# First block of one token tile, late first global queries, held weight joins, and stacked value parts in an attention and MLP kernel

## The chip, the cores and the metric

The kernel runs on one core of a Trainium2 chip. The metric is the device time of one execution in microseconds, as the median over runs. The core has TensorE (PE; its weight loads are listed apart as PEld), VectorE (DVE), ScalarE (ACT), GpSimd (POOL) and SyncE (SP), which here issues every data transfer.

## The reference

Sparse attention is followed by a two-layer MLP, both in float32 (the MLP weights arrive as 64-bit floats).

```
# 8 sequences b, 8 heads, 512 local tokens (l), 32 global tokens (g), head size 64
k_all = concat([k_g, k_l]); v_all = concat([v_g, v_l])
out_g = softmax(q_g @ k_all.T / 8) @ v_all          # a global query sees all 544 keys
s_ll  = where(|i - j| <= 32, q_l @ k_l.T / 8, -1e9)  # a local query sees a band
out_l = softmax(concat([q_l @ k_g.T / 8, s_ll])) @ concat([v_g, v_l])
x = heads of concat([out_g, out_l]) side by side     # 8 * 544 = 4352 tokens x 512
h = x @ w_in                                         # 512 -> 2048
return (h * sigmoid(h)) @ w_out                      # 2048 -> 512
```

## The kernel before

The 4352 tokens are 34 tiles of 128: for each half of the sequences, four sequences of four local tiles (chunk `c` of 0 to 3 in sequence `b`), and one tile with the global tokens of these four sequences. `SIZES` groups the tiles into blocks for the MLP: 2, ten times 3, and 2.

**MLP.** `first_layer(n, f)` makes 128 of the 2048 hidden columns for all tiles of block n, in PSUM tile `h`; ACT (tanh) and DVE make the activation; `second_layer(n, f)` adds its product with `w_out` to one PSUM bank `out` per tile. f runs over 16, and the second layer of a pass comes after the first layer of the next. Block 0 multiplies whole float32 values (`w_32`, `xh`). From block 1 on, each operand is split in a high part (rounded to fp32r, a faster form of TensorE) and a low part (the rest), and three products are made for one: high·high, high·low, low·high (L563, L588 to L590).

**Weights.** `load_weights` (L164) takes half of one f's weights: SP fetches 512 KB of 64-bit words into `raw_w` (a ring of eight), ACT makes the float from the upper word (L179), DVE shifts the lower word (L181) and joins both (L182). `split_weights` (L185) makes `w_hi` on ACT (L192) and `w_lo` on POOL (L193). It is called in block 0's `second_layer`, after the last use of the whole weights of that f. `LOOK` and `FIRSTW` set how many passes ahead the loading runs.

**Attention** comes in 128 steps, k = 16 b + 4 c + pr, each of two heads (u) and one local tile:

- `st_load`, `st_vload` fetch queries, keys and values; `st_split`, `st_vsplit` split them;
- `st_scores` makes the scores `s` on PE and the softmax on DVE and ACT into `probs`; split steps send these through a DMA into `rr`, which gives them the fp32r type;
- `st_turn` transposes them on PE into `t`, from where ACT and DVE write `pt` (or `pt_hi`, `pt_lo`). Beside the 128 columns of local queries stand 32 columns of global queries, which POOL copies from `pgt` (L398 to L402);
- `st_out` multiplies values and `pt` into PSUM tile `o`: 160 columns are 128 local and 32 global queries (L423). A split step makes, for each head and each half `a` of the keys, three products on 64 stationary columns: `vhi`·`pt_hi`, `vlo`·`pt_hi` and `vhi`·`pt_lo`. ACT copies the high part to `xh` (L434), DVE the rest to `xl` (L435) and the sum over chunks of the global part to `acc` (L440, L442).

Steps below `KF` = 24 work on whole float32 values in transposes and outputs, and below 24 also in the scores; steps 24 to 27 (`ND` = 28) split a compact layout in which the two heads are stacked on the 128 rows.

**Global queries.** For sequence b, `g_load`, `g_split`, `g_scores` (tile `gs`, four pairs of heads), `g_soft` (softmax in `pgs`) and `g_turn` (transposes into `pgt`, parts `gt` and `gu`) have to be through before the turns of that sequence's steps. Below `GF` = 2 they are whole float32; later ones go through a DMA (`g_move`, tiles `rg`). For sequence 0 they come at the very start; for b + 1, in the middle of b's steps.

**Order.** `put` gives each part of each step a due time, the list `stream` is sorted by it, and `advance` issues parts up to a time. Before block 0, everything that its tiles need is issued (`AHEAD` = 4 steps a tile), with more PSUM banks (`early`). Afterwards `fill`, called between groups of MLP products, issues the next block's attention in proportion to the work done. PE keeps the order of the program. The other engines' and SP's order comes from a planner that works from modelled times; `tc.keep_in_program_order` puts an instruction behind everything traced before it on its engine. Before, this holds for the first eight weight transfers only.

## Time and profile before

| | us |
|---|---|
| median of three runs | 1089.91 (1088.55 to 1090.19) |
| profiled execution | 1086.34 |
| its span, first to last instruction | 1084.6 |
| PE busy | 1053.5 (97%) |
| DVE busy | 727.4 (67%) |
| ACT busy | 693.0 (64%) |
| POOL busy | 146.5 (14%) |

In the profile a row of a group reads: line, engine, operation, output<-inputs with their shapes, count, then busy time, mean ns of one, and the engine's idle time ahead of them with what ended it. Matmuls overlap in the pipeline, so that the mean of one is longer than the spacing between two; the spacing is read from the chain of work or from the starts in the timeline. A float32 product shows as two PE instructions, a fp32r product as one.

### The profile page before, as it was taken

What the parts mean: (1) busy time and instruction counts of PE and PEld (TensorE: products, weight loads), DVE (VectorE), ACT (ScalarE), POOL (GpSimd) and SP (SyncE); (2) the same over time, 40 slices, a digit from 0 to 9 for tenths busy, and PEclk for the clock granted to TensorE, in tenths of its full rate; (3) what the DMA queues carried; (4) which work ended last, traced back from release to release, by engine and by line L of the source; (5) the groups of instructions that cost most, each with busy time, mean ns of one, the idle gap of its engine ahead of it and who ended that gap; (6) DMA issues with size and microseconds to landing.
All of it is one profiled execution on the core that took longest, in us unless ns stands there. A gap on an engine that the chain in (4) does not pass through costs nothing.

```text
span 1084.6 us, 20466 instructions
## 1 busy us (share of the span) xinstructions
PE 1053.5 (97%) x6568; PEld 934.9 (86%) x6568; DVE 727.4 (67%) x2367; ACT 693.0 (64%) x1845; POOL 146.5 (14%) x360
## 2 busy tenths in 40 slices
PE   6878999999999999999999999999999999999998
PEld 4645778989999999999999999998999999999997
DVE  5974355777677777666777877786778867753322
ACT  7875456767677766656766766776677776653232
POOL 3123542111100110000110100001000111000000
PEclk8989999999999999999999999999999999999999
DMA  9961112343334333332433433443344433310000
GB/s 351 380 189 59 57 59 76 119 146 125 111 112 142 124 107 115 116 115 82 140 110 122 149 111 109 138 135 108 111 141 125 141 114 112 112 60 20 1 30 20
DMA packets 69611, 127.29 MB, mean 117 GB/s; under 512 B 9344, under 2 KB 29312, under 8 KB 69504
## 3 DMA queue, kind: packets, MB, share of 16 engines
q1 hardware_dynamic: 69504, 125.99, 36.1%
...
## 4 chain that ended last, share of the span: by engine, by line
PE 93%; ACT 3%; DVE 2%; issue 1%; DMA 1%; ACTq 0%; DVEq 0%
PE h L563 33%; PE out L588 12%; PE out L590 11%; PE out L589 11%; PE o L423 10%; PE s L345 6%; PE t L380 3%; PE h L557 2%; PE out L586 2%; PE t L378 1%; DMA raw_w<-in_wts_dram 1%; PE gs L226 1%; PE gs L228 1%; ACT w_hi L192 1%; ACT w L179 1%
## 5 line engine op out<-in xcount | busy, mean ns | idle before, releaser
L563 PE MATMUL h<-xh,w_hi 128*128 128x384 f32 (+1 forms) x704 | 236.8, 336 | 0.0
L563 PE MATMUL h<-xh,w_lo 128*128 128x384 f32 (+1 forms) x704 | 233.5, 332 | 0.0
L563 PE MATMUL h<-xl,w_hi 128*128 128x384 f32 (+1 forms) x704 | 233.1, 331 | 0.0
L569 ACT ACTIVATE t<-h 128x384 f32<-128x384 f32 (+1 forms) x192 | 90.7, 472 | 207.3 <-PE h L563 189.4
L588 PE MATMUL out<-w_hi,gh 128*128 128x512 f32 x512 | 210.6, 411 | 0.0
L590 PE MATMUL out<-w_hi,gl 128*128 128x512 f32 x512 | 201.3, 393 | 0.0
L589 PE MATMUL out<-w_lo,gh 128*128 128x512 f32 x512 | 200.3, 391 | 0.0
L571 DVE SCALAR_TENSOR_TENSOR t<-t,h 128x384 f32<-128x384 f32 (+1 forms) x176 | 95.2, 541 | 132.6 <-ACT t L569 131.9
L563 PEld LDWEIGHTS h<-xl,w_hi 128*128 128x128 f32 x704 | 132.6, 188 | 5.4 <-issue 0.5
L563 PEld LDWEIGHTS h<-xh,w_hi 128*128 128x128 f32 x704 | 132.5, 188 | 5.4 <-issue 0.7
L400 POOL CAST pt_hi<-pgt 128x64 fp32r<-128x64 f32 (+1 forms) x132 | 39.1, 308 | 724.4 <-PE o L423 706.1
L563 PEld LDWEIGHTS h<-xh,w_lo 128*128 128x128 f32 x704 | 132.3, 188 | 0.0
L576 DVE TENSOR_TENSOR gl<-t,gh 128x384 fp32r<-128x384 f32 (+1 forms) x176 | 96.8, 550 | 46.6 <-PE out L590 42.5
L349 DVE CUSTOM_DVE_ANT_0 probs<-s,mask 128x224 f32<-128x224 f32 x244 | 85.0, 384 | 62.0 <-PE s L345 61.4
L353 ACT ACTIVATE probs<-probs,st 128x224 f32<-128x224 f32 x244 | 115.7, 475 | 11.2 <-DVE st L349 10.5
L590 PEld LDWEIGHTS out<-w_hi,gl 128*128 128x128 f32 x512 | 96.1, 188 | 22.3 <-DVE gl L576 0.3
L589 PEld LDWEIGHTS out<-w_lo,gh 128*128 128x128 f32 x512 | 97.0, 189 | 10.5
L588 PEld LDWEIGHTS out<-w_hi,gh 128*128 128x128 f32 x512 | 96.4, 188 | 10.6 <-ACT gh L575 0.4
L575 ACT CAST gh<-t 128x384 fp32r<-128x384 f32 (+1 forms) x176 | 88.3, 501 | 21.8 <-DVE t L571 17.3
L434 ACT CAST xh<-o 64x128 fp32r<-64x128 f32 x240 | 61.3, 256 | 42.5 <-PE o L423 29.4
L312 ACT CAST qk<-raw 128x704 fp32r<-128x704 f32 x100 | 78.2, 782 | 15.9 <-PE s L345 15.6
L435 DVE TENSOR_TENSOR xl<-o,xh 64x128 fp32r<-64x128 f32 x240 | 67.3, 280 | 30.9 <-ACT xh L434 27.4
...
## 6 DMA issues: line engine op xcount, KB each, us to landing
raw<-in_qk_dram SPq DMA_DIRECT2D x100, 352.0 KB, 3.0
rr<-probs SPq DMA_DIRECT2D x104, 256.0 KB, 2.3
raw_w<-in_wts_dram SPq DMA_DIRECT2D x32, 512.0 KB, 6.3
vraw<-in_v_dram SPq DMA_DIRECT2D x128, 128.0 KB, 2.4
...
```

The costliest lines, as they stand in the source:

```text
L312: nc.scalar.copy(out=qk, in_=raw)
L349: nc.vector.tensor_tensor_reduce(out=p[:, u, :W], in0=s[:, u * W : (u + 1) * W], in1=mask_of[c], scale=-SCALE, scalar=3.0e38, op0=ALU.add, ...
L353: nc.scalar.activation(p[:, u, :W], p[:, u, :W], AF.Exp, bias=st[:, u : u + 1], scale=-1.0, accum_out=st[:, 2 + u : 3 + u])
L423: nc.tensor.matmul(o[:D, u * wide : u * wide + m], v[:, a, u, :], pt[:, u, a, :m], start=(i == 0), stop=(i == len(terms) - 1))
L563: nc.tensor.matmul(h[:, :nt], wt, x[:, c, :nt], start=(i == 0), stop=(i == 3 * NCC - 1))
L569: nc.scalar.activation(t[:, :nt], h[:, :nt], AF.Tanh, scale=0.5)
L571: nc.vector.scalar_tensor_tensor(out=out[:, :nt], in0=t[:, :nt], scalar=1.0, in1=h[:, :nt], op0=ALU.add, op1=ALU.mult)
L575: nc.scalar.copy(out=gh[:, :nt], in_=t[:, :nt])
L576: nc.vector.tensor_tensor(out=gl[:, :nt], in0=t[:, :nt], in1=gh[:, :nt].bitcast(F32), op=ALU.subtract)
L588: nc.tensor.matmul(o, gh[:, sl], wh, start=(f == 0), stop=False)
L589: nc.tensor.matmul(o, gh[:, sl], wl, start=False, stop=False)
L590: nc.tensor.matmul(o, gl[:, sl], wh, start=False, stop=(f == NF - 1))
```

## The change

- `SIZES`: block 0 has one tile, then eleven blocks of three.
- Sequence 0's global queries leave the start. They are issued after the first four steps (`LATE`); steps 0 to 3 make only their local outputs, and `g_late` makes the global part of these four steps afterwards, in eight products of 32 columns.
- Weights: `fetch_weights` and `join_weights` are apart, `FETCH` = 4 and `LOOK` = 2 passes ahead; every transfer, join and split is held in the order of the program. Splits leave `second_layer`: the split of f stands at pass 11 + f, counted from block 0's first.
- Values: `vv` holds both parts side by side, [high, low]. For each head and half, one product of 128 stationary columns with `pt_hi` and one of 64 with `pt_lo`. `st_out` copies rows 64 to 127 of `o` (the low part's product) to `xs` (ACT), adds rows 0 to 63 (DVE), and then makes `xh` (ACT) and `xl` (DVE) for both heads at once; POOL sums `acc`.
- Steps 16 to 23 leave whole float32 in transposes and outputs (`KF` = 16); the scores of steps below 28 are whole, so that 24 to 27 are not split. Sequence 2's global queries become whole float32 (`GF` = 3).
- The last 32 keys of the global queries are transposed straight from `pgs` and split into `pgh` and `pgl`, in place of the second `rg` transfer.

```diff
...
-SIZES = (2, 3, 3, 3, 3, 3, 3, 3, 3, 3, 3, 2)
+SIZES = (1,) + (3,) * 11
 BUFS = dict(qk=2, raw=2, p=2, vraw=2, rr=1)
 ND = 28
-KF = 24
-GF = 2
+KF = 16
+GF = 3
 KP = 12
 SCRATCH = 8
-LOOK = 5
-FIRSTW, PACE, WAT = 2, 1.0, -1.5
+FETCH, LOOK = 4, 2
+SPLIT0, SPLITS = 11, 1.0
+FIRSTW = {1: 2, 2: 1, 3: 1}
+FIRSTC = {2: 1, 3: 1}
+LATE = dict(load=-1.0, first=0.2, head=0.8, soft=0.3, turn=1.0, slot=4.0)
...
-MOVE0, TURN0 = (0.1, 0.8), (1.5, 3.6)
-START = dict(head=0.55, gap=0.0, late=-0.65, first=1.8)
...
+    w_32, w_hi, w_lo, w_raw, w_next = [], [], [], [], [0, 0]
+
+    hold = tc.keep_in_program_order
+
+    def fetch_weights():
+        i = w_next[0]
+        w_next[0] += 1
+        sl = slice(DM * (i % 2), DM * (i % 2 + 1))
+        w_raw.append(scratch(SCRATCH + i % (NF - SCRATCH), I32, f"raw_w{i}"))
+        load = nc.sync.dma_start(out=w_raw[i], in_=wts[i // 2, :, sl].bitcast(I32))
+        hold(load)
+
+    def join_weights():
+        i = w_next[1]
+        w_next[1] += 1
+        while w_next[0] <= i:
+            fetch_weights()
+        f = i // 2
+        sl = slice(DM * (i % 2), DM * (i % 2 + 1))
+        if f + 1 == NF:
+            w_32.append(work.tile([P, SKV], F32, tag="klo", bufs=BUFS["qk"], name=f"w{i}")[:, :DM])
+        elif i % 2 == 0:
+            w = const.tile([P, 2 * DM], F32, tag=f"ws{f + 1}", name=f"w{f}")
+            w_32.extend((w[:, :DM], w[:, DM:]))
...
-        nc.vector.tensor_scalar(out=low, in0=low, scalar1=29, scalar2=None, op0=ALU.logical_shift_right)
-        nc.vector.scalar_tensor_tensor(out=wi, in0=wi, scalar=3, in1=low, op0=ALU.logical_shift_left,
-                                       op1=ALU.bitwise_or)
+        hold(nc.vector.tensor_scalar(out=low, in0=low, scalar1=29, scalar2=None, op0=ALU.logical_shift_right))
+        hold(nc.vector.scalar_tensor_tensor(out=wi, in0=wi, scalar=3, in1=low, op0=ALU.logical_shift_left,
+                                            op1=ALU.bitwise_or))
 
     def split_weights(f):
         taken.add(f)
@@ -188,9 +202,9 @@
         w_lo.append(const.tile([P, 2 * DM], F32R, tag=f"ws{f}", name=f"w_lo{f}"))
         for c0 in range(0, 2 * DM, DM):
             sl = slice(c0, c0 + DM)
-            hi, lo, w = w_hi[f][:, sl], w_lo[f][:, sl], w_32[f][:, sl]
-            nc.scalar.copy(out=hi, in_=w)
-            nc.gpsimd.tensor_tensor(out=lo, in0=w, in1=hi.bitcast(F32), op=ALU.subtract)
+            hi, lo, w = w_hi[f][:, sl], w_lo[f][:, sl], w_32[2 * f + c0 // DM]
+            hold(nc.scalar.copy(out=hi, in_=w))
+            hold(nc.gpsimd.tensor_tensor(out=lo, in0=w, in1=hi.bitcast(F32), op=ALU.subtract))
 
 
...
-        r1 = two.tile([P, SG], F32R, tag="rg", name=f"rg1_{b}_{hh}")
         nc.sync.dma_start(out=r0.bitcast(F32), in_=pgs[hh][:, : 4 * P])
-        nc.sync.dma_start(out=r1.bitcast(F32), in_=pgs[hh][:, 4 * P :])
-        state["rg", hh] = r0, r1
+        state["rg", hh] = r0
...
-            state["pgt"] = work.tile([P, 5, H, SG], F32, tag="pgt", name=f"pgt{b}")
-        pgt = state["pgt"]
+
+            state["pgt"] = (work.tile([P, NC, H, SG], F32, tag="pgt", name=f"pgt{b}"),
+                            work.tile([P, QG], F32R, tag="pgh", name=f"pgh{b}"),
+                            work.tile([P, QG], F32R, tag="pgl", name=f"pgl{b}"))
+        pgt, pgh, pgl = state["pgt"]
...
-        nc.tensor.transpose(tb[:SG, :P] if whole else tb[:SG, :P].bitcast(F32R), r1, idt)
-        nc.scalar.copy(out=pgt[:SG, 4, hs, :], in_=tb[:SG, :P].rearrange("p (h q) -> p h q", h=4))
+        nc.tensor.transpose(tb[:SG, :P], pgs[hh][:, 4 * P :], ident.bitcast(F32))
+        for i in range(2):
+            rows, src = slice(SG * (2 * hh + i), SG * (2 * hh + i + 1)), tb[:SG, QG * i : QG * (i + 1)]
+            nc.scalar.copy(out=pgh[rows, :], in_=src)
+            nc.vector.tensor_tensor(out=pgl[rows, :], in0=src, in1=pgh[rows, :].bitcast(F32), op=ALU.subtract)
...
-        if k < KF and k % 2:
-            vraw = two.tile([P, 2, 2, D], F32, tag="vhi" if k % 4 == 1 else "vlo", name=f"vraw{k}")
+        if k < NPR:
+            vraw = scratch(k, F32, f"vraw{k}")[:, : 4 * D].rearrange("p (a u d) -> p a u d", a=2, u=2)
+        elif k < KF and k % 2:
+            vraw = two.tile([P, 2, 2, 2, D], F32, tag="vv", name=f"vraw{k}")[:, 0]
...
-        if k < ND:
-            n = QW + W
-            nc.scalar.copy(out=qk[:, :n], in_=raw[:, :n])
-            (nc.gpsimd if k < ND else nc.vector).tensor_tensor(out=klo[:, :n], in0=raw[:, :n], in1=qk[:, :n].bitcast(F32), op=ALU.subtract)
-            return
         nc.scalar.copy(out=qk, in_=raw)
-        (nc.gpsimd if k < ND else nc.vector).tensor_tensor(out=klo[:, :KW], in0=raw[:, QW:], in1=qk[:, QW:].bitcast(F32), op=ALU.subtract)
+        nc.vector.tensor_tensor(out=klo[:, :KW], in0=raw[:, QW:], in1=qk[:, QW:].bitcast(F32), op=ALU.subtract)
...
-        vhi = two.tile([P, 2, 2, D], F32R, tag="vhi", name=f"vhi{k}")
-        vlo = two.tile([P, 2, 2, D], F32R, tag="vlo", name=f"vlo{k}")
+        vv = two.tile([P, 2, 2, 2, D], F32R, tag="vv", name=f"vv{k}")
+        vhi, vlo = vv[:, :, :, 0, :], vv[:, :, :, 1, :]
         nc.scalar.copy(out=vhi, in_=vraw)
         (nc.gpsimd if k < ND else nc.vector).tensor_tensor(
             out=vlo, in0=vraw, in1=vhi.bitcast(F32), op=ALU.subtract)
-        tiles["v", k] = vhi, vlo
+        tiles["v", k] = vv
...
-            if k < KF:
+            if k < ND:
                 terms = [(raw[:, qs], raw[:, QW : QW + W])]
-            elif k < ND:
-                ks = slice(QW, QW + W)
-                terms = [(qk[:, qs], qk[:, ks]), (qk[:, qs], klo[:, ks]), (klo[:, qs], qk[:, ks])]
             else:
...
+        if k < NPR:
+
+            pt = tiles["pt", k] = pt_whole(k)
+            nc.scalar.copy(out=pt[:, :, :, :P], in_=t4)
+            return
+        did(("last", b) if (c, pr) == (NC - 1, NPR - 1) else k, ("turn", b, pr // 2))
+        pgt, pgh, pgl = state["pgt"]
+        g = pgt[:, c, 2 * pr : 2 * pr + 2, :]
         if whole:
             pt = tiles["pt", k] = pt_whole(k)
+            nc.scalar.copy(out=pt[:, :, :, :P], in_=t4)
+            nc.gpsimd.tensor_copy(out=pt[:, :, 0, P:], in_=g)
             if c == NC - 1:
+                rows = slice(SG * pr, SG * (pr + 1))
+                hi, lo = (part.bitcast(F32)[rows, :].rearrange("p (u q) -> p u q", u=2) for part in (pgh, pgl))
                 nc.gpsimd.memset(pt[:, :, 1, P:], 0.0)
-            nc.scalar.copy(out=pt[:, :, :, :P], in_=t4)
...
+        pt_hi, pt_lo = pt_tiles(k)
+        nc.scalar.copy(out=pt_hi[:, :, :, :P], in_=t4)
+        nc.vector.tensor_tensor(out=pt_lo[:, :, :, :P], in0=t4, in1=pt_hi[:, :, :, :P].bitcast(F32),
+                                op=ALU.subtract)
+        nc.gpsimd.tensor_copy(out=pt_hi[:, :, 0, P:], in_=g)
+        nc.gpsimd.tensor_tensor(out=pt_lo[:, :, 0, P:], in0=g, in1=pt_hi[:, :, 0, P:].bitcast(F32),
+                                op=ALU.subtract)
+        if c == NC - 1:
+            for pt, part in ((pt_hi, pgh), (pt_lo, pgl)):
+                src = part[SG * pr : SG * (pr + 1), :].rearrange("p (u q) -> p u q", u=2)
+                nc.gpsimd.tensor_copy(out=pt[:SG, :, 1, P:], in_=src)
...
+            if k < NPR:
+                tiles["late", k] = vraw
         else:
-            vhi, vlo = tiles.pop(("v", k))
+            vv = tiles.pop(("v", k))
...
         for u in range(2):
-            if whole:
-                terms = [(vraw, pt_f, a) for a in range(2)]
-            else:
-                terms = [(v, pt_hi, a) for a in range(2) for v in (vhi, vlo)] + [(vhi, pt_lo, a) for a in range(2)]
-            for i, (v, pt, a) in enumerate(terms):
-                m = wide if a == 0 or c == NC - 1 else P
-                nc.tensor.matmul(o[:D, u * wide : u * wide + m], v[:, a, u, :], pt[:, u, a, :m],
-                                 start=(i == 0), stop=(i == len(terms) - 1))
-        g0 = SG * (b % 4)
+            for a in range(2):
+                m = wide if (a == 0 or c == NC - 1) and k >= NPR else P
+                at = slice(u * wide, u * wide + m)
+                if whole:
+                    nc.tensor.matmul(o[:D, at], vraw[:, a, u, :], pt_f[:, u, a, :m], start=(a == 0), stop=(a == 1))
+                    continue
+
+
+                nc.tensor.matmul(o[:, at], vv[:, a, u].rearrange("p t d -> p (t d)"), pt_hi[:, u, a, :m],
+                                 start=(a == 0), stop=(a == 1))
+                nc.tensor.matmul(o[:D, at], vv[:, a, u, 0], pt_lo[:, u, a, :m], start=False, stop=(a == 1),
+                                 skip_group_check=(a == 1))
...
+        xs = work.tile([P, wide], F32, tag="xs", name=f"xs{k}")
         for u in range(2):
+            at = slice(u * wide, (u + 1) * wide)
             rows = slice(D * u, D * (u + 1))
...
-            if c == 0:
-                nc.vector.tensor_copy(out=gdst, in_=gsrc)
-            else:
-                nc.vector.tensor_tensor(out=gdst, in0=gsrc, in1=gdst, op=ALU.add)
+            nc.scalar.copy(out=xs[rows, :], in_=o[D:, at])
+            nc.vector.tensor_tensor(out=xs[rows, :], in0=o[:D, at], in1=xs[rows, :], op=ALU.add)
+        nc.scalar.copy(out=xh[:, pr, sl], in_=xs[:, :P])
+        nc.vector.tensor_tensor(out=xl[:, pr, sl], in0=xs[:, :P], in1=xh[:, pr, sl].bitcast(F32), op=ALU.subtract)
+        if c == 0:
+            nc.gpsimd.tensor_copy(out=gdst, in_=xs[:, P:])
+        else:
+            nc.gpsimd.tensor_tensor(out=gdst, in0=xs[:, P:], in1=gdst, op=ALU.add)
+
+    def g_late():
+
+        pgt = state["pgt"][0]
+        o = attbank("o", "late")
+        for pr in range(NPR):
+            vraw = tiles.pop(("late", pr))
+            for u in range(2):
+                at = SG * (NPR * u + pr)
+                nc.tensor.matmul(o[:D, at : at + SG], vraw[:, 0, u, :], pgt[:, 0, 2 * pr + u, :], start=True, stop=True)
+        for u in range(2):
+            nc.vector.tensor_copy(out=acc[D * u : D * (u + 1), :, :SG],
+                                  in_=o[:D, P * u : P * (u + 1)].rearrange("p (n q) -> p n q", n=NPR))
...
-                xblk[n] = (two.tile([P, NPR, 3 * P], F32, tag="xh", name="x_0"),
-                           two.tile([P, NPR * 3 * P], F32, tag="xl", name=f"w{NF - 1}"))
+                xblk[n] = two.tile([P, NPR, 3 * P], F32, tag="xh", name="x_0"), None
...
-    for h in range(NPR):
-        due = START["head"] * h + (START["late"] if h > 1 else 0.0)
-        put(due - 0.6, g_load, 0, h)
-        put(due, g_split, 0, h)
-        put(due + START["gap"], g_scores, 0, h)
-        if h % 2:
-            put(due + START["gap"] + 0.2, g_soft, 0, h // 2)
-    at = START["first"]
     AHEAD = NPR * SIZES[0]
     for k, (t, b, c, pr) in enumerate(steps):
         a = (k, b, c, pr)
         j = k % NST
         lag = LAG if k < AHEAD else 0.0
         if k == AHEAD:
-            at += LAG
-        if j == 0:
+            at += LAG + LATE["first"]
+            for h in range(NPR):
+                due = at + LATE["head"] * h
+                put(due + LATE["load"], g_load, 0, h)
+                put(due, g_scores, 0, h)
+                if h % 2:
+                    put(due + LATE["soft"], g_soft, 0, h // 2)
+                    put(due + LATE["soft"], g_move, 0, h // 2)
+                    put(due + LATE["soft"] + LATE["turn"], g_turn, 0, h // 2)
+            at += LATE["slot"]
+            put(at + DUE["turn"] - 0.1, g_late)
+        if j == 0 and b:
             for hh in range(2):
-                put(at + (MOVE if b else MOVE0)[hh], g_move, b, hh)
-                put(at + (TURN if b else TURN0)[hh], g_turn, b, hh)
-        if FIRSTW <= k < AHEAD:
-            for i in range(int((k + 1) * PACE) - int(k * PACE)):
-                put(at + WAT, load_weights)
+                put(at + MOVE[hh], g_move, b, hh)
+                put(at + TURN[hh], g_turn, b, hh)
+        for counts, fn in ((FIRSTW, fetch_weights), (FIRSTC, join_weights)):
+            for i in range(counts.get(k, 0)):
+                put(at + DUE["load"], fn)
...
-        if n == 0:
-            split_weights(f)
...
-                while tuple(w_next) < (min(NF, f + LOOK), 0):
-                    load_weights()
+                while w_next[1] < 2 * min(NF, f + LOOK):
+                    join_weights()
+                while w_next[0] < 2 * min(NF, f + FETCH):
+                    fetch_weights()
             elif f == 0:
                 advance(ends[n])
                 now[:] = n, 0
+            while len(w_hi) < NF and SPLIT0 + SPLITS * len(w_hi) <= NF * n + f:
+                split_weights(len(w_hi))
...
```

76 lines of the change are left out of this document (28 added, 48 removed).

## The prediction

> **What bounds the kernel now.** I read the page's totals and slices first, then the busy time by stretch, the chain of work that ended last, and the groups of instructions. The page:
>
> ```profile
> span 1084.6 us, 20466 instructions
> PE 1053.5 (97%) x6568; PEld 934.9 (86%) x6568; DVE 727.4 (67%) x2367; ACT 693.0 (64%) x1845; POOL 146.5 (14%) x360
> PEclk8989999999999999999999999999999999999999
> GB/s 351 380 189 59 57 59 76 119 146 125 111 112 142 124 107 115 116 115 82 140 110 122 149 111 109 138 135 108 111 141 125 141 114 112 112 60 20 1 30 20
> PE 93%; ACT 3%; DVE 2%; issue 1%; DMA 1%; ACTq 0%; DVEq 0%
> ```
>
> PE owns 93% of the chain; the other 7% has to lie where the clock is under 9 and DMA is high, the first slices. Boundaries are in the instruction timeline: the first product, block 0's first `h` (L557), block 1's first `h` (L563), the last product.
>
> ```profile
> 3.81 6.16 PE L226 MATMUL gs<-raw_g 128*64 128x272 f32 x16 [3.81 <-DMA raw_g<-in_gqk_dram]
> 47.66 2.27 PE L557 MATMUL h<-x,w 128*128 128x256 f32 x8
> 154.86 0.74 PE L563 MATMUL h<-xh,w_hi 128*128 128x384 f32 x1
> 1079.64 0.40 PE L590 MATMUL out<-w_hi,gl 128*128 128x512 f32 x1
> ```
>
> Busy time by stretch (us, then busy time and count for PE, PEld, DVE, ACT, POOL, then clock, DMA share, GB/s), then a piece of the chain and the weights' row of the DMA issues (size, us to landing):
>
> ```profile
> 0.00:90.10 90.10, 66.89 (x290) 46.82 (x290) 65.93 (x212) 72.11 (x183) 21.55 (x46) 0.89 0.81 286
> 0.00:154.90 154.90, 130.47 (x573) 92.03 (x573) 97.21 (x329) 103.35 (x277) 51.25 (x82) 0.92 0.54 187
> 154.90:249.90 95.00, 94.75 (x599) 84.43 (x598) 62.66 (x211) 64.19 (x172) 21.02 (x42) 1.00 0.35 111
> 82.09 3.94 DMA raw_w<-in_wts_dram
> raw_w<-in_wts_dram SPq DMA_DIRECT2D x32, 512.0 KB, 6.3
> ```
>
> So there are two regimes. Up to 90 us no engine is full: ACT, the busiest, stands at 72.1/90.1 = 80%, DVE at 73%, and the chain passes through weights that land late. From block 1 on, PE is full and ACT and DVE have a third to spare: there only PE's own work counts.
>
> **The change, part by part.** I split the time at T1, block 1's first `h` (154.9 now), and cost "after T1" in PE issue time, "before T1" by the busiest engine.
>
> PE prices come from the chain (start, us, what): first six pieces in block 0 (fp32, two tiles), then the steady state, then one pass over f of the two-tile last block; timeline rows give the start-to-start spacing of `gs` and `out`.
>
> ```profile
> 98.47 1.06 PE gs L226 x4
> 103.22 0.76 PE s L345 x4
> 103.98 1.73 PE h L557 x8
> 105.71 0.44 PE t L378 x4
> 106.14 1.72 PE out L586 x4
> 107.86 1.23 PE o L423 x8
> 505.01 0.89 PE o L423 x12
> 506.63 2.11 PE h L563 x12
> 509.43 0.29 PE t L380 x4
> 513.68 0.44 PE s L345 x4
> 514.81 0.80 PE o L423 x12
> 602.34 0.31 PE L228 MATMUL gs<-qk_g 128*64 128x272 f32 x1
> 603.10 0.39 PE L588 MATMUL out<-w_hi,gh 128*128 128x512 f32 x1
> 605.15 0.24 PE L423 MATMUL o<-pt_hi,vhi 128*64 128x160 f32 x1
> 1072.62 1.43 PE h L563 x12
> 1075.44 1.43 PE h L563 x12
> ```
>
> An fp32 step costs 0.76 + 0.44 + 1.23 = 2.43 us of PE; a split step now 0.44 + 0.29 + 0.80 = 1.53 (0.09 more in the last chunk of a sequence, where all twelve `o` products are wide). A three-tile f costs 2.11 + (605.15 - 603.10) = 4.16, a two-tile f 1075.44 - 1072.62 = 2.82, a two-tile fp32 f 1.73 + 1.72 = 3.45.
>
> *After T1.*
> - Blocks: ten of three tiles and one of two become eleven of three: 176 x 4.16 - (160 x 4.16 + 16 x 2.82) = +21.4.
> - `o` with `vv`: twelve products become eight, four on 128 columns. No row has a 128-column stationary block with 160 moving columns. Below it is the 64-column spacing, 0.80/12 = 0.067; above, `s` (128 columns, 224 moving), 0.44/4 = 0.11. The f32r `t` has 128 stationary and 128 moving columns at 0.29/4 = 0.073; between it and `s`, in proportion to columns, 160 lands at 0.085, which I take, since `t` is nearest. A step is then 2 x (0.085 + 0.074 + 0.073 + 0.060) = 0.58, call it 0.59, against 0.80: -0.21, and about -0.24 in a last chunk. For the 100 steps from 28 on (28 of them last chunks): -(72 x 0.215 + 28 x 0.245) = -22.3. Between the bounds: -27 to -10.
> - Four more steps lie behind T1 (twenty before it now, sixteen then): fp32 `s`, f32r `t`, new `o`: 4 x (0.76 + 0.29 + 0.59) = +6.6. Steps 20 to 23 leave fp32: 4 x (1.64 - 2.43) = -3.2. Steps 24 to 27 get fp32 scores for six f32r products of the `s` spacing: 4 x (0.76 - 0.67 - 0.21) = -0.5.
> - Global queries of sequence 2 become fp32: 4 x (1.06 - 0.76) = +1.2, with 0.76 = 603.10 - 602.34; fp32 transposes there and of the 32-column ends, and sequence 1's turn that now falls behind T1: about +2.
>
> Sum after T1: +5.2, so 1080.0 - 154.9 + 5.2 = 930.3 us from T1 to the last product; the end after it stays at 4.5.
>
> Cover for what is priced at nothing. `st_out` gives ACT three copies for two (L434's 0.256 each, some longer for 160 columns: +0.3 per step, 31 us in all), gives POOL the sum into `acc`, and leaves DVE level: two sums and one subtraction for 2 x 0.280 + 2 x 0.173. PE hides it: steps lie some 7 us apart, and `o`'s bank is free after two copies and two sums, as soon as now. Uncovered it would cost 0.3 us a step. Steps 16 to 23 gain splits and an `rr` transfer each (eight on SP); in return steps 24 to 27 and four global heads lose theirs, and SP loses the small `rg1` transfers. Some 22 of 32 weight splits move into block 1: 22 x 0.579 = 12.7 us for ACT, 22 x 1.30 = 28.7 for POOL, five passes ahead of use. On ACT's 64.2 of 95 us that makes 81%: still covered, with a few us at risk.
>
> ```profile
> L181 DVE TENSOR_SCALAR raw_w<-raw_w 128x512 uint32<-128x512 uint32 x32 | 16.3, 508 | 11.2 <-DMA raw_w<-in_wts_dram 10.8
> L182 DVE SCALAR_TENSOR_TENSOR w<-w,raw_w 128x512 uint32<-128x512 uint32 x32 | 23.7, 747 | 3.7 <-ACT w L179 2.8
> L571 DVE SCALAR_TENSOR_TENSOR gh<-t,h 128x256 f32<-128x256 f32 x16 | 6.7, 417 | 14.5 <-ACT t L569 14.4
> L435 DVE TENSOR_TENSOR xl<-o,xh 64x128 fp32r<-64x128 f32 x240 | 67.3, 280 | 30.9 <-ACT xh L434 27.4
> L442 DVE TENSOR_TENSOR acc<-o,acc 64x32 f32<-64x32 f32 x192 | 33.3, 173 | 0.2
> L434 ACT CAST xh<-o 64x128 fp32r<-64x128 f32 x240 | 61.3, 256 | 42.5 <-PE o L423 29.4 <-DVE acc L442 4.1 <-DVE acc L440 4.0
> L192 ACT CAST w_hi<-w 128x512 fp32r<-128x512 f32 x32 | 18.5, 614 | 4.8 <-DVE w L182 3.5 <-PE s L345 1.3
> L193 POOL TENSOR_TENSOR w_lo<-w,w_hi 128x512 fp32r<-128x512 f32 x32 | 41.1, 1304 | 47.5 <-PE out L586 29.6 <-ACT w_hi L192 17.8
> L345 PEld LDWEIGHTS s<-klo,qk 128*128 128x128 f32 x208 | 39.6, 190 | 1.7
> L423 PEld LDWEIGHTS o<-pt_hi,vlo 128*64 128x64 f32 x416 | 56.2, 135 | 6.6
> ```
>
> One rule speaks against the `o` term. The Trainium skill, page "TensorE: Matmul & The Clock Gate", section "LDWEIGHTS (loading the stationary operand)", makes a load's time the column count over 1.2 GHz, whatever the rows: 107 ns for 128 columns, 53 for 64. As an estimate by that page, eight loads in series would need 4 x 160 ns = 0.64 us a step for 0.59, some 4 us more in all. The trace does not bear it out fully: the `t` products above come every 73 ns with a 128-column load each.
>
> *Before T1.* Joining weights stays at 32 halves: 16.3 + 23.7 = 40 us of DVE. DVE now does 97.2; take off 40.0 and 6.7 for `gh`, and 50.5 is left for twenty steps and two sequences' global softmax: at most 2.5 a step, I take 2.2. Four steps go (-8.8); the first four write no `acc` (-4 x 0.35); steps 4 to 7 gain `xl` (+1.1); one-tile `gh` saves some 0.13 x 16 = 2.1; `g_late`'s copies and the `pgl` pieces add 1.2. DVE: 87. ACT: 103.4 - 4 x 2.3 - 12.7 (splits) - about 1 = 81. PE: sixteen f at 1.73 (half of 3.45) = 27.7, sixteen steps at 2.43 = 38.9, `gs` 8 x 1.06 = 8.5, turns and `g_late` about 2: 77. DMA: 32 x 0.52 MB of weights, sixteen steps and eight global heads are 25 MB, 68 us at the 370 GB/s of the first slices. DVE is the longest. If the busiest engine again runs at the 80% of the first 90 us, T1 = 87/0.80 = 108.
>
> The moves behind that: block 0 needs four steps instead of eight and no global queries, so its first `h` should come near 25 us for 47.7. Holding puts each weight transfer, join and split behind everything traced before it on SP, ACT, DVE and POOL. Queued behind a held join that still waits for its transfer would be the steps' DVE and ACT work, and PE behind that in its fixed order; transfers are issued two f ahead of their join, some 10 us against 6.3 to landing, so I price that wait at nothing (uncovered: one landing, about 4 us, as in the chain's row above). The global queries of sequence 0 now pass SP behind the first step loads and weights; their late turn is due before step 4's turn, which needs it.
>
> **Sum.** 108 + 930.3 + 4.5 = 1042.8 of span, 1.74 more outside (1086.34 against 1084.6): 1044.5 on the profiled scale, -41.8. The runs shown have a median of 1089.91, 3.57 above the profiled one: 1048.
>
> **Rivals** (on the scale of the median).
> - *The start shortens less.* Block 0 took (154.9 - 47.7)/16 = 6.7 us an f; per f, joins and steps are the same, only PE's part shrinks. From 25 us on at 6.7, T1 = 132: 1072. For it: ACT and DVE bounded the first 90 us. Against: after 90 us PE set the pace, with one tile less to do now.
> - *The start shortens more.* DVE at 90%: T1 = 96, 1036. For it: the joins in a fixed order stop splits from running ahead of softmax. Against: DVE and ACT wait on each other within each join.
> - *The wide block saves little.* PEld shows 190 ns for a 128-column load and 135 for 64. If each 128-column product takes `s`'s 0.11, the step is 0.71, and 104 x 0.12 is lost: 1060.
> - *Slower.* The output chain copy, sum, copy, subtract stops PE: if PE in its fixed order waited for `o`'s bank through ACT and DVE queues at every step, 104 split steps would pay. The gain of 41.6 is gone from 0.40 us a step on; one copy and one sum exposed twice, 2 x (0.28 + 0.31) = 1.2, makes 1170. Against it stand 7 us between steps and an idle third of both engines.
>
> **How the numbers follow.** Forecast 0.56 (1040 to 1060), smaller start gain 0.17, larger 0.13, wide block without gain 0.08, slower 0.04, no difference 0.02. From 1034 to 1073 takes in the forecast, both bounds of `o`, the smaller gain and half of the larger. A difference of 0.2%, 2.2 us, is about what a measurement of this kernel can tell; all cases but the last two are far beyond it.
>
> **What would show it.** Block 1's first f32r `h` near 108 us and block 0's first `h` near 25; from there to the last product some 930 us at a full PE; `o` in x8 pieces of 0.58 to 0.64; DVE the busiest before T1. Wrong would be: PE idle in steady state, released by the output's copies or sums; `raw_w` landings still on the chain; `o` pieces near 0.7; or block 1 stretched beyond 92 us by late `w_lo`.

## The result, and the profile after

The change made the kernel slower: 1096.95 us median (1095.1 to 1097.75, four runs) against 1089.23 us for the kernel before on the same chip (1088.0 to 1090.19, four runs), a ratio of 1.0075 with a 95% interval of 1.0063 to 1.0087. The prediction was 1048 us, 41 us faster. The profiled execution took 1097.75 us, its span 1096.0.

The page of the kernel after: the span, the totals of the engines, the granted TensorE clock in 40 slices, and the shares of the chain that ended last.

```profile
span 1096.0 us, 19915 instructions
PE 1043.7 (95%) x6168; PEld 932.9 (85%) x6168; DVE 749.5 (68%) x2285; ACT 734.9 (67%) x1977; POOL 190.6 (17%) x480
PEclk9999898999999999999999999999999999999999
PE 87%; DVE 4%; ACT 4%; issue 2%; DMA 1%; POOL 0%; SPq 0%; ACTq 0%; DVEq 0%; POOLq 0%
```

PE is busy 9.8 us less than before (1053.5 then), but its share of the chain fell from 93% to 87%. The time went into waits: DVE and ACT hold 8% of the chain, 5% before.

The same boundaries as in the prediction, from PE's timeline of the kernel after: block 0's first `h`, block 1's first `h` (T1), the last product.

```profile
30.96 0.82 PE L606 MATMUL h<-x,w 128*128 128x128 f32 x5
132.63 0.67 PE L612 MATMUL h<-xh,w_hi 128*128 128x384 f32 x1
1089.34 0.39 PE L639 MATMUL out<-w_hi,gl 128*128 128x512 f32 x1
```

| us | before | after | forecast |
|---|---|---|---|
| block 0's first `h` | 47.7 | 31.0 | 25 |
| T1 | 154.9 | 132.6 | 108 |
| T1 to last product | 924.8 | 956.7 | 930.3 |
| last product to end of span | 4.9 | 6.7 | 4.5 (from the last product's end) |

T1 came down by 22.3 us of the forecast 46.9, and the rest grew by 31.9 us instead of 5.2.

Busy time by stretch, kernel after (columns as in the prediction):

```profile
0.00:31.00 31.00, 21.12 (x73) 14.85 (x73) 8.74 (x37) 13.01 (x34) 5.67 (x22) 1.00 0.85 299
31.00:103.00 72.00, 59.00 (x336) 42.20 (x335) 54.75 (x188) 51.16 (x144) 9.44 (x20) 0.98 0.75 241
103.00:132.60 29.60, 16.63 (x88) 12.63 (x89) 19.64 (x65) 17.84 (x51) 13.70 (x19) 0.87 0.18 54
0.00:132.60 132.60, 96.76 (x494) 69.68 (x495) 83.13 (x288) 82.00 (x229) 28.81 (x60) 0.96 0.65 213
132.60:230.90 98.30, 95.10 (x531) 84.79 (x530) 57.12 (x172) 67.93 (x183) 46.10 (x67) 0.95 0.29 88
```

Up to T1 DVE did 83.1 us of work (87 forecast) and was busy 63% of the time instead of 80%. Between 103 and 132.6 us nothing is full: PE stands at 56%, DVE at 66%, DMA at 18%. There is no busiest engine to divide by; something is waiting for something else. The view of waits on PE says for what (total us, times, longest):

```profile
PE o L444 <- DVE acc L464: 8.9, 3, 7.3
PE s L357 <- DMA raw<-in_qk_dram: 7.6, 4, 3.4
PE gt L291 <- issue: 5.2, 7, 2.0
PE gt L291 <- DVE acc L464: 4.7, 2, 2.4
PE gs L240 <- DVE xs L471: 2.9, 1, 2.9
PE gs L240 <- DVE acc L464: 2.5, 1, 2.5
```

`DVE acc L464` is the last DVE sum that reads `o`'s PSUM bank, which `gt` and half of `gs` use too. PE waits 16.1 us for it (8.9 + 4.7 + 2.5), all before T1. The longest, from the timeline of DVE, ACT and PE:

```profile
103.49 1.57 DVE L196 SCALAR_TENSOR_TENSOR w<-w,raw_w 128x512 uint32<-128x512 uint32 x1
...
106.82 1.22 ACT L193 ACTIVATE w<-raw_w 128x512 f32<-128x512 f32 x2
...
107.93 1.13 ACT L206 CAST w_hi<-w 128x512 fp32r<-128x512 f32 x2
...
109.09 0.26 ACT L459 CAST xh<-o 64x128 fp32r<-64x128 f32 x1
109.20 1.56 DVE L196 SCALAR_TENSOR_TENSOR w<-w,raw_w 128x512 uint32<-128x512 uint32 x1
110.78 0.28 DVE L461 TENSOR_TENSOR xl<-o,xh 64x128 fp32r<-64x128 f32 x1
110.98 0.17 DVE L464 TENSOR_TENSOR acc<-o,acc 64x32 f32<-64x32 f32 x1
111.41 1.83 PE L444 MATMUL o<-pt,vraw 128*64 128x160 f32 x6 [7.27 <-DVE acc L464]
```

The sum that frees the bank takes 0.17 us. It stands in DVE's queue behind weight joins (L196) and softmax, and behind `xl`, which needs ACT's copy `xh`. That copy stands in ACT's queue until 109.09, behind softmax, two joins (L193) and two splits (L206); then DVE is in a join until 110.76. PE, next in its fixed order to write the same bank, stands still for 7.27 us. A single PSUM bank and two in-order queues make the wait; no engine is full.

### The profile page after: what moved, and what is told of

Read it like the earlier page. It is cut to its first block, busy times and chain, and to the rows that moved or that the text cites. A ratio compares the mean times of both kernels' runs of the same rounds, so it can differ in the third digit from the quotient of the medians.

```text
span 1096.0 us, 19915 instructions
## 1 busy us (share of the span) xinstructions
PE 1043.7 (95%) x6168; PEld 932.9 (85%) x6168; DVE 749.5 (68%) x2285; ACT 734.9 (67%) x1977; POOL 190.6 (17%) x480
## 4 chain that ended last, share of the span: by engine, by line
PE 87%; DVE 4%; ACT 4%; issue 2%; DMA 1%; POOL 0%; SPq 0%; ACTq 0%; DVEq 0%; POOLq 0%
PE h L612 33%; PE out L637 11%; PE out L639 11%; PE out L638 11%; PE s L357 5%; PE o L448 4%; PE o L450 3%; PE t L392 3%; PE o L444 2%; DVE w L196 1%; PE gs L240 1%; PE gt L291 1%; ACT probs L365 1%; ACT w_hi L206 1%; DMA raw<-in_qk_dram 1%
## 5 line engine op out<-in xcount | busy, mean ns | idle before, releaser
L612 PE MATMUL h<-xh,w_hi 128*128 128x384 f32 x704 | 242.4, 344 | 0.0
L612 PE MATMUL h<-xl,w_hi 128*128 128x384 f32 x704 | 239.2, 340 | 0.0
L612 PE MATMUL h<-xh,w_lo 128*128 128x384 f32 x704 | 239.0, 339 | 0.0
L637 PE MATMUL out<-w_hi,gh 128*128 128x512 f32 x528 | 219.6, 416 | 0.0
L620 DVE SCALAR_TENSOR_TENSOR t<-t,h 128x384 f32<-128x384 f32 x176 | 97.2, 552 | 112.7 <-ACT t L618 111.5
L625 DVE TENSOR_TENSOR gl<-t,gh 128x384 fp32r<-128x384 f32 x176 | 99.2, 563 | 46.0 <-PE out L639 40.2
L365 ACT ACTIVATE probs<-probs,st 128x224 f32<-128x224 f32 x244 | 115.8, 476 | 12.2 <-DVE st L361 10.9
L416 POOL CAST pt_hi<-pgt 128x64 fp32r<-128x64 f32 x112 | 38.0, 339 | 491.8 <-PE o L450 349.6
L624 ACT CAST gh<-t 128x384 fp32r<-128x384 f32 x176 | 89.9, 511 | 22.2 <-DVE t L620 19.5
L471 DVE TENSOR_TENSOR xs<-o,xs 64x160 f32<-64x160 f32 x224 | 70.7, 316 | 28.8 <-ACT xs L470 24.6
L448 PE MATMUL o<-pt_hi,vv 128*128 128x160 f32 x448 | 87.6, 264 | 0.6 <-DVE xs L471 0.3
```

The costliest lines, as they stand in the source:

```text
L365: nc.scalar.activation(p[:, u, :W], p[:, u, :W], AF.Exp, bias=st[:, u : u + 1], scale=-1.0, accum_out=st[:, 2 + u : 3 + u])
L448: nc.tensor.matmul(o[:, at], vv[:, a, u].rearrange("p t d -> p (t d)"), pt_hi[:, u, a, :m], start=(a == 0), stop=(a == 1))
L612: nc.tensor.matmul(h[:, :nt], wt, x[:, c, :nt], start=(i == 0), stop=(i == 3 * NCC - 1))
L620: nc.vector.scalar_tensor_tensor(out=out[:, :nt], in0=t[:, :nt], scalar=1.0, in1=h[:, :nt], op0=ALU.add, op1=ALU.mult)
L624: nc.scalar.copy(out=gh[:, :nt], in_=t[:, :nt])
L625: nc.vector.tensor_tensor(out=gl[:, :nt], in0=t[:, :nt], in1=gh[:, :nt].bitcast(F32), op=ALU.subtract)
```

## The experiments

Each ratio is to the kernel before on the same chip, with its 95% interval. T1 and first `h` are read from each run's timeline as above, from one profile a run.

Four of the profiles (the kernel after, and the runs below without stacked values, with the other order of `o`, and with 64 columns for 128) have the same instructions in the same order on PE, DVE, ACT, POOL and SP up to T1. Their T1 are 132.6, 134.3, 130.5 and 135.2, their first `h` 31.0, 30.7, 27.6 and 31.0. PE idles 32.5 to 33.7 us in each of them after its first product; what differs is how long PE runs at half speed. So a difference of less than 5 us between two T1, or 3.4 us between two first `h`, is not shown by one profile each; the medians and PE's idle time decide there.

### Which part of the change costs, and which pays

**Stacked values alone**, in the kernel before: the new `vv` tile and output chain, and the straight transposes of the last 32 global keys; blocks, global queries and weights as before.

```
-   terms = [(v, pt_hi, a) for a in range(2) for v in (vhi, vlo)] + [(vhi, pt_lo, a) for a in range(2)]
+   nc.tensor.matmul(o[:, at], vv[:, a, u].rearrange("p t d -> p (t d)"), pt_hi[:, u, a, :m], ...)
+   nc.tensor.matmul(o[:D, at], vv[:, a, u, 0], pt_lo[:, u, a, :m], ...)
```

> The kernel before with only the value parts side by side (one product on 128 columns and one on 64, the new output chain, and the straight transposes of the last 32 global keys that make room for it); blocks, weights and global queries as before. Theory: in the changed kernel a pair of o products took 0.186 us at 160 columns and 0.159 at 128, so a step takes 0.69 us for 0.80, and PE is full from block 1 on: 104 steps save some 11 us, about 1078 (ratio 0.990). Rival: the longer output chain keeps the o bank busy and gives it back in stalls: 1087 to 1092.

Measured: 1075.36 us, 0.9884 (0.9865 to 0.9903). T1 151.4; `o` takes 75.6 us after T1 for 90.4 before (from the start-to-start spacing of its products). This part pays, but 14.8 us instead of 22.

**The change without stacked values**: `o` with three 64-column products a term again, everything else as after.

```
-   nc.tensor.matmul(o[:, at], vv[:, a, u].rearrange("p t d -> p (t d)"), pt_hi[:, u, a, :m], ...)
+   terms = [(v, pt_hi, a) for a in range(2) for v in (vhi, vlo)] + [(vhi, pt_lo, a) for a in range(2)]
```

> The changed kernel with three products on 64 columns and the output chain of before in all split steps. Theory (the stacked parts are worth some 12 us, 112 split steps): 1108 to 1110. Rival (stalls of the new output chain take as much as the products save): 1095 to 1099.

Measured: 1105.23 us, 1.0157 (1.0138 to 1.0175), T1 134.3. What remains of the change costs 1.6% by itself; stacking gives 0.8% of it back.

**Blocks alone**, in the kernel before.

```
-SIZES = (2, 3, 3, 3, 3, 3, 3, 3, 3, 3, 3, 2)
+SIZES = (1,) + (3,) * 11
```

> The kernel before with only the block sizes of the change (one tile, then eleven blocks of three); weights, global queries and value parts as before. The changed kernel without its value parts ran at 1.0157 of before. Theory (the short first block is what costs: PE gains 27.6 us of products before block 1 but waits there for weights and softmax, and pays 21 us after): block 1 starts at 130 to 140, and the time is above before, 1095 to 1110. Rival (what costs is the late global queries and the held order, not the block): below before, 1075 to 1086.

Measured: 1100.11 us, 1.0109 (1.0094 to 1.0124). T1 136.3, block 0's first `h` at 37.3, T1 to last product 957.7. `h` and `out` after T1 take 750.9 us for 728.4: +22.5, where the prediction's first term has +21.4. T1 fell by only 18.6. The tile leaves a stretch in which PE loses a fifth of its time to waits and half speed (34 of 154.9 us, worked out below) and comes back where PE is full. This move alone is a loss.

### What sets T1

**Joins without DVE**: DVE's two operations on each weight half are left out, so the weights lack their lower bits.

```
-   hold(nc.vector.tensor_scalar(out=low, in0=low, scalar1=29, ...))
-   hold(nc.vector.scalar_tensor_tensor(out=wi, in0=wi, scalar=3, in1=low, ...))
```

> The changed kernel without the two DVE operations of each join (the lower bits of the weights are left out; the float comes from the upper word alone), 64 operations and 36 us of DVE less before block 1. If DVE's work sets the time before block 1 (as the prediction had it), block 1 starts near (83 - 36)/83 of 132.6, at 75 to 95. If the start is bound by chains between engines (scores, softmax, transpose, output one after the other) and the first 31 us stay as they are, it starts at 105 to 120.

Measured: 1087.71 us, 0.9998 (0.9987 to 1.0008); T1 124.02. Busy time up to T1 in that run:

```profile
0.00:124.00 124.00, 95.56 (x494) 69.09 (x495) 50.05 (x224) 81.53 (x229) 26.00 (x60) 0.97 0.68 227
```

DVE's 83.1 us became 50.05, and T1 moved by 8.6, less than either expectation had it; PE's idle time before T1 fell by 7.7. An engine that loses 33 us and gives 9 is not the bound. This ends the prediction's 87/0.80.

**More PSUM banks for `o`** in block 0: the banks `out1` and `out2`, which a one-tile block doesn't use, take turns with `o`'s, for `gt` and that half of `gs` too.

```
+        if first0 and not early and kind == "o":
+            i = next(banks[kind]) % 3
+            if i:
+                return ps_out.tile([P, 512], F32, tag=f"out{i}", name=name)
```

> The changed kernel with three PSUM banks in turn for o (and for the global tiles that use o's bank) as long as block 0 runs, which leaves two of the three out banks unused. Before block 1 PE stood 16 us waiting for o's bank (4.1 up to 103 us, 12.0 behind it), released by the sum into acc at the end of DVE's queue. Theory (one bank is the cause): these waits go, block 1 starts at 117 to 122 for 132.6, 1082 to 1088. Rival (DVE's and ACT's queues are the cause, and PE waits for the next thing in them): block 1 at 128 to 132, 1092 to 1097.

Measured: 1080.37 us, 0.9921 (0.9903 to 0.9939). In its timeline and by stretch:

```profile
117.47 0.42 PE L617 MATMUL h<-xh,w_hi 128*128 128x384 f32 x1
```

```profile
31.00:103.00 72.00, 61.62 (x360) 45.23 (x360) 61.37 (x209) 55.51 (x160) 15.46 (x26) 1.00 0.73 239
0.00:117.50 117.50, 91.55 (x495) 65.99 (x495) 81.93 (x285) 81.02 (x228) 30.43 (x60) 0.99 0.71 237
```

T1 132.6 to 117.5 with DVE's work unchanged (81.9 for 83.1), and no wait for `acc` left: 16.1 us became none. PE's idle time before T1 fell from 32.5 to 22.5 us. The other 5 us are mostly half speed, which alone differs by up to 6 us between the four like profiles above. So the bank, not DVE's capacity, cost block 0 these 10 us; with the medians 16.6 us apart, the gain itself is far beyond that spread. In this run too one step's last sum comes 12.7 us after its last `o` product, and PE does not wait for it. The Trainium skill's page "Perfetto Trace Analysis", section "Matmuls", says that independent matmul groups should rotate through different PSUM banks so that emptying one overlaps the next group; this run agrees: T1 comes 15.1 us earlier, with 10.0 us less idle time.

**Free order**: joins and splits no longer held to the written order (their transfers still are).

```
-    hold = tc.keep_in_program_order
+    hold = lambda ins: ins
```

> The changed kernel with joins and splits of the weights free for the planner to order (their transfers still held). Theory: from 104 to 111 us PE waits 7.3 us for o's bank, whose release on DVE stands behind a held join, and smaller waits are of the same kind; free, block 1 starts near 118 instead of 132.6: 1080 to 1086. Rival: what costs is the work itself (DVE and ACT full, POOL's subtraction beside DVE's), and the order does not matter: 1094 to 1099. Another rival: splits run ahead of the softmax again: above 1099.

Measured: 1100.59 us, 1.0126 (1.0099 to 1.0153). First `h` 26.9, T1 135.8; PE's idle time before T1 is 30.7 us for 32.5. My theory that holding was what delayed block 0 fell: by the ratios the free order is 0.5% slower. **The same with three banks**:

```
+   (three banks for o, as above)
-    hold = tc.keep_in_program_order
+    hold = lambda ins: ins
```

> The changed kernel with three banks for o in block 0, and joins and splits free for the planner. With one bank, freeing them gave 1100 for 1097. Theory (the held order is neither good nor bad, the bank was): 1078 to 1083. Rival (held joins keep softmax ahead of splits, and that is worth 5 us or more): 1085 to 1092.

Measured: 1088.19 us (1082.8 to 1092.08), 0.9998 (0.9984 to 1.0012), T1 125.8 for 117.5. By the medians holding is worth some 8 us there; where they come from is open, since the idle time before T1 is nearly the same (23.6 us for 22.5) and the rest of the 8.3 us at T1 is half speed.

**Weights behind the step loads**: the first four weight transfers issued behind the queries and keys of steps 0 to 2, still ahead of step 3's, and no join before block 0, because steps 1 to 3 wait 2.96, 0.60 and 0.61 us for `raw`.

```
-FIRSTW = {1: 2, 2: 1, 3: 1}
-FIRSTC = {2: 1, 3: 1}
+FIRSTW = {3: 4}
+FIRSTC = {}
```

> The changed kernel with the first weight transfers issued behind the queries and keys of steps 0 to 2 instead of between them (four halves ahead of step 3's load, no join before block 0). Theory: the scores of steps 1 to 3 wait 2.96, 0.60 and 0.61 us for their transfer, which stands behind weight transfers; without that, block 0 starts 4 us earlier, block 1 2 to 4: 1093 to 1095. Rival (weights are late instead, and the joins set the pace): 1097 to 1102.

Measured: 1102.84 us, 1.0138 (1.0121 to 1.0155); first `h` 32.2, T1 137.4. It fell: step 3's scores now wait 5.99 us for their transfer, and the first join ends at 32.2 us, where PE has waited 3.85 us for it.

**Later splits**: more weight splits pushed into block 1.

```
-SPLIT0, SPLITS = 11, 1.0
+SPLIT0, SPLITS = 16, 0.8
```

> The changed kernel with the splits of the weights later (first at pass 16 instead of 11, 0.8 passes apart instead of 1), so that none falls into block 0. Theory: DVE's joins at 96 to 111 us took 1.5 us instead of 0.69 while POOL made w_lo, and ACT's held splits stand ahead of the output copies; without them block 1 starts some 6 to 10 us earlier, but the splits fall just ahead of their use: 1088 to 1094. Rival (the splits only move their cost into block 1, where PE then waits for w_lo): 1097 or more.

Measured: 1110.86 us, 1.0201 (1.0176 to 1.0227); T1 129.5, but block 1 now waits. PE's waits between 129 and 250 us in that run:

```profile
PE h L612 <- ACT w_hi L206: 7.6, 4, 3.0
PE h L612 <- POOL w_lo L207: 5.7, 5, 3.1
```

13.3 us of waits in block 1, for 4.5 us less idle time before T1. In the kernel after, with SPLIT0 at 11, the view of waits has neither row.

### Half speed in the first 30 us

Step 0's four `s` instructions take 1.86 us, for 1.02 at 100.49 us, while the granted clock of 0 to 31 us says 1.00. The trace has no clock record ahead of 29.17 us, and the view counts that time as 1.00; at the record products change to twice their pace. The four like profiles have this first record at 29.2, 28.0, 20.6 and 28.6 us, so its place is in part chance. **Dummy products of 64 columns** fill PE's gaps in the first four steps.

```
+            nc.tensor.matmul(dst, ident.bitcast(F32), ident.bitcast(F32)[:, : 2 * SG], start=True, stop=True)
...
+            warm(s[:, 2 * W :], 14 if k == 0 else 4)
```

> The changed kernel with products of no use on PE in the gaps of the first four steps (10 ahead of the first scores, 14 behind them, 4 behind each other scores, 5 ahead of each output; the identity, 64 columns, into unused columns). In the first 31 us all products took twice their later time (scores 1.86 us for 0.76, outputs 1.97 for 1.0), 11 us in all. Theory (PE runs at half speed because it idles in between): with the gaps filled they run at full speed, block 0 starts 3 to 7 us earlier, 1089 to 1094. Rival (the start hangs on transfers, softmax and copies, and PE's speed hides behind them): 1095 to 1099.

Measured: 1105.47 us, 1.015 (1.0129 to 1.017), first `h` 38.8, T1 142.4, slower than either expectation. **Three dense products** of 480 columns behind step 0's scores, with three banks:

```
+                nc.tensor.matmul(dense[:, : QW + W], raw[:, :P], raw[:, : QW + W], start=True, stop=True)
```

> The changed kernel with three banks for o in block 0 (1080), and behind the scores of step 0 three dense products of no use (float32, 480 moving columns, some 5 us at half speed). In the kernels that begin with the global scores (272 columns, back to back) full speed came at 6.6 to 9 us; in the changed one, with gaps, only at 20 to 29; with small products of 64 columns in the gaps at 30. Theory (PE's speed follows how densely the array is used in the last few us): full speed from about 10 us on, block 0 starts 3 to 6 us earlier, 1074 to 1078. Rival (speed comes at its own time, or the start hangs on transfers): 1080 to 1084.

Measured: 1081.73 us, 0.994 (0.9926 to 0.9953), T1 120.5: no better than three banks alone (0.9921). PE's timeline, first in the run with 64-column dummies, then in that with dense ones:

```profile
1.86 4.53 PE L305 MATMUL s<-ident 128*128 128x64 f32 x20 [1.86 <-DVE ident L88]
13.64 1.81 PE L363 MATMUL s<-raw 128*128 128x224 f32 x4
26.26 1.97 PE L454 MATMUL o<-pt,vraw 128*64 128x128 f32 x8
30.31 1.09 PE L454 MATMUL o<-pt,vraw 128*64 128x128 f32 x8
```

```profile
3.47 1.86 PE L362 MATMUL s<-raw 128*128 128x224 f32 x4 [3.47 <-DMA raw<-in_qk_dram]
5.12 3.37 PE L366 MATMUL dense<-raw 128*128 128x480 f32 x6
8.32 0.92 PE L362 MATMUL s<-raw 128*128 128x224 f32 x4
...
15.84 1.97 PE L453 MATMUL o<-pt,vraw 128*64 128x128 f32 x8 [0.68 <-ACT pt L406]
```

Small products without a gap left PE at half speed until 29 us; dense ones brought full speed at about 7 us, and it was lost again by 14 us, after waits of 1.3 and 1.4 us between its products. Half speed costs the kernel after some 10 us before 31 us (PE runs 19.2 of the first 29.2 us, at half its later pace); neither run made up for it.

### What `o` costs

**Other order**: both 128-column products of a bank first, then both of 64 columns, so that the two widths alternate half as often.

```
+                spans.append((m, at))
...
+            for a, (m, at) in enumerate(spans):
+                    nc.tensor.matmul(o[:D, at], vv[:, a, u, 0], pt_lo[:, u, a, :m], ...)
```

> The changed kernel with the four products of a head in another order: both on 128 columns first, then both on 64. If what costs is the change from a 128-column to a 64-column product (start to start 0.111 after the wide one, 0.075 after the narrow one), half of the changes go and some 0.07 us a step is saved: about 1089. If each wide product costs a fixed time of loading 128 columns, which is not hidden under 128 to 160 moving columns, the order changes nothing: 1096 to 1098, o some 0.69 us a step.

Measured: 1096.67 us, 1.0087 (1.0068 to 1.0106); `o` after T1 76.8 us for 77.1. Alternating costs nothing. **64 columns for 128**: the stacked product replaced by one with the high part alone, so the values' low part is left out.

```
-   nc.tensor.matmul(o[:, at], vv[:, a, u].rearrange("p t d -> p (t d)"), pt_hi[:, u, a, :m], ...)
+   nc.tensor.matmul(o[:D, at], vv[:, a, u, 0], pt_hi[:, u, a, :m], start=(a == 0), stop=False)
```

> The changed kernel with the product on 128 columns replaced by one on the 64 columns of the high part (the product of the low part is left out, the output chain reads the high rows twice), so that the count of products, their moving columns and the chain stay. If the load of 128 columns is what makes a pair take 0.186 (160 columns) and 0.159 (128), pairs now take 0.150 and 0.125 and a step 0.55 us: 112 steps save some 15 us, about 1081. If it is the number of products or the accumulation into the same rows, o stays at 0.69 and the time at 1096.

Measured: 1086.53 us, 0.9982 (0.9968 to 0.9996); `o` after T1 62.7 us, 14.4 less, with as many products of the same moving width. The 128 stationary columns cost 14.4/448 = 32 ns for each of the 448 products. The gain in the total was less, because PE then waited 10.3 us for `xs` at L291 (0.3 in the kernel after).

### Putting together what pays

**The kernel before with stacked values, steps 16 to 23 split in transposes and outputs, and scores split only from step 28**, and the same **with two banks for `o` in block 0**:

```
-KF = 24
+KF = 16
-        if k < KF:
+        if k < ND:
```

> The kernel before with the value parts side by side (as in the first of these runs, 1075) and, beside that, steps 16 to 23 split and the scores of steps 24 to 27 whole, as in the change. Theory: PE saves 8 x 0.76 us on transposes and outputs and loses 4 x 0.09 on scores, steps 20 to 27 in a full PE: 1069 to 1072. Rival (the splits load ACT and POOL where the weights are still being split, so that it is given back): 1074 to 1078.

```
+        if first0 and not early and kind == "o" and next(banks[kind]) % 2:
+            return ps_out.tile([P, 512], F32, tag="out2", name=name)
```

> The kernel before with the value parts side by side, steps 16 to 23 split, the scores of steps 24 to 27 whole (1074.6), and beside that two banks in turn for o in block 0 (one out bank is unused there). Up to 90 us PE waited 3.3 us for o's bank in the kernel before, and 1.8 with the value parts. Theory (few waits for it, since PE has more to do): 1071 to 1075. Rival (waits in a chain go with it, as in the changed kernel): 1064 to 1069.

Measured: 1074.61 us, 0.9866 (0.985 to 0.9882), T1 150.3; with the second bank 1063.88 us, 0.9782 (0.9767 to 0.9797), T1 139.5. The page's chain of the last:

```profile
span 1061.8 us, 19921 instructions
PE 93%; ACT 2%; DVE 2%; issue 2%; DMA 1%; SPq 0%; POOL 0%; ACTq 0%; DVEq 0%; POOLq 0%
```

The steps from 16 on add nothing clear to stacked values alone (0.9866 for 0.9884, with intervals that overlap). With the second bank it beats both kernels, with two tiles in block 0. The free bank was there before the change too, and moves T1 by 10.8 us even under two tiles, the medians by 10.7; PE's idle time before T1 falls from 20.4 to 15.5 us.

## Why the prediction was wrong

The missing 53 us of span (1042.8 forecast, 1096.0 measured) are T1 with +24.6, the time after T1 with +26.4 and the end with the rest.

**"If the busiest engine again runs at the 80% ... T1 = 87/0.80 = 108"** is the step that failed first. The amount of DVE work was right (83.1 for 87), the division wrong. The 80% was ACT's share of the first 90 us; up to T1 the kernel before has DVE at 97.2 of 154.9 us, 63%, as the kernel after does. Splitting PE's time before T1 gives the table below. Idle time is read between products; half of the time in which PE runs at a granted clock of 0.5 (or ahead of the trace's first clock record, which products show to be half speed) is counted as excess.

| before T1, us | PE's products at full speed | PE idle | excess of half speed |
|---|---|---|---|
| before | 117.1 | 20.6 | 13.3 |
| after | 83.4 | 32.5 | 13.4 |
| after, three banks | 84.2 | 22.5 | 7.3 |

The remainder to T1 is the start of the first product. PE's work fell by 34 us, as the change asked. Waiting and half speed together did not fall with it: 34 us before, 46 after, 30 with three banks. T1 is PE's work plus such a remainder, and of the 34 us saved 12 went into new waits. The smaller start gain (T1 = 132) was among the rivals, and its number came, but by luck: it had 16 passes of 6.7 us from 25 us on, and there were 16 of 6.35 from 31.0 on. Of the reason given for it ("ACT and DVE bounded the first 90 us"), the run without DVE's joins excludes a DVE bound; ACT's work was not taken out in any run.

**"`o`'s bank is free after two copies and two sums, as soon as now"** failed with it. It was written for the steps after T1; before T1 the prediction had no price for the bank at all, though block 0 keeps the old output chain. From a step's last `o` product to its last sum 1.7 to 5.5 us pass in the kernel before, and 1.7 to 4.3 in the kernel after but for one step with 10.9, the one shown above. PE also comes back to the bank sooner, having one tile less of `h` and `out` between two `o`; how much of the waits this makes is not shown. The kernel before waited 3.3 us for `acc` before T1, the kernel after 16.1. The rival on the slower side had this mechanism ("PE ... waited for `o`'s bank through ACT and DVE queues") but put it at the 104 split steps after T1 at a price per step; most of it sat in block 0 instead and was not what alone made the kernel slower.

**`o` with `vv`** was mis-sized, within its bounds. 112 steps at 0.59 are some 67 us; 77.1 were measured, 0.69 a step. One step in the timeline of the kernel after, with the loads left out:

```profile
174.69 0.24 PE L448 MATMUL o<-pt_hi,vv 128*128 128x160 f32 x1
...
174.76 0.24 PE L450 MATMUL o<-pt_lo,vv 128*64 128x160 f32 x1
...
174.83 0.26 PE L448 MATMUL o<-pt_hi,vv 128*128 128x128 f32 x1
...
175.35 0.44 PE L637 MATMUL out<-w_hi,gh 128*128 128x512 f32 x1
```

From the first `o` to the first `out` 0.66 us pass. I took the `t` row (73 ns) as nearest for a 128-column stationary block; the transposes' spacing does not carry over. The rival of the wide block (0.71 a step) was nearly right in its price. The Trainium skill's page "TensorE: Matmul & The Clock Gate", section "LDWEIGHTS (loading the stationary operand)", by which I had estimated 0.64, was nearer than the row I preferred; its difference between 128 and 64 columns is 53 ns, where the run with 64 columns shows 32.

**Blocks**: +21.4 forecast. Blocks alone gave +22.5; in the kernel after `h` and `out` take 760.1 us for 728.4, +31.7. Of the 10 beyond the forecast some 5 are half speed around waits; the other 5 are not explained. **Covers "priced at nothing"** after T1: PE is idle 10.2 us for 2.1. One of these waits, in the timeline of the kernel after, and the clock in the stretches around it:

```profile
176.78 1.14 ACT L206 CAST w_hi<-w 128x512 fp32r<-128x512 f32 x2
177.94 0.58 ACT L413 CAST pt_hi<-t 128x512 fp32r<-128x512 f32 x1
178.42 0.52 ACT L624 CAST gh<-t 128x384 fp32r<-128x384 f32 x1
178.83 0.38 ACT L245 COPY pg<-gs 64x272 f32<-64x272 f32 x1
179.23 0.29 ACT L470 COPY xs<-o 64x160 f32<-64x160 f32 x1
...
180.01 1.14 PE L240 MATMUL gs<-raw_g 128*64 128x272 f32 x2 [2.86 <-DVE xs L471]
```

```profile
176.00:180.00 4.00, 1.16 (x8) 0.53 (x7) 1.79 (x4) 3.54 (x10) 4.00 (x6) 0.92 0.18 68
180.00:184.00 4.00, 3.98 (x9) 2.61 (x10) 0.29 (x1) 0.58 (x2) 1.86 (x3) 0.50 0.33 92
184.00:188.00 4.00, 4.00 (x23) 4.00 (x22) 0.79 (x2) 0.55 (x2) 0.24 (x1) 0.73 0.00 0
```

`xs`, the copy that the change adds, stands behind two moved splits and three other copies, and `gs` waits for the bank that `xs` empties. PE waits 2.86 us and then runs at a granted clock of 0.50 and 0.73 for 4 us each, which costs 4 x 0.50 + 4 x 0.27 = 3.1 us more. Another 5.2 us stand in the view of waits at `gt` with no releaser (`issue`, seven times). Each of them ends 0.10 or 0.11 us after DVE's sum of `o` into `xs` (L471):

```profile
383.60 0.32 DVE L471 TENSOR_TENSOR xs<-o,xs 64x160 f32<-64x160 f32 x1
...
384.02 0.64 PE L291 MATMUL gt<-ident,rg 128*128 128x128 f32 x4 [1.96 <-issue]
```

By these times `gt` waits for the same bank, and 8.7 of the 10.2 us are waits for it. This is the prediction's own sign of being wrong, "PE idle in steady state, released by the output's copies or sums". The new chain is only part of it: without stacked values PE is idle 7.0 us after T1, and the same `gs` waits 2.2 us for the old chain's sum. I had taken ACT at 81% in block 1 as "still covered, with a few us at risk". It stood lower, at 67.9 of 98.3 us or 69%, and its queue still was not free when it mattered: a share says nothing about the order.

After T1 the miss adds up as `o` +10.0, blocks +10.3, idle PE +8.1, other products -1.7: +26.7, for 26.4.

**Right** were: the first block's tile costing 21 us after T1, DVE's amount of work, the order of the first `h` (31 for 25; `raw` transfers, 4.2 us, and half speed lie in between, but no run shows what they cost), splits as a risk to block 1 (shown by the later splits). Not explained in full is the 1.6% of the change without stacked values against 1.1% of the blocks alone; the moved global queries are in it, and were not tried by themselves. What bounds T1 at 117.5 with three banks is open as well: 22.5 us of PE's idle time have no single releaser.
